# A sigmoid first on ScalarE, w_in's passes placed behind chosen sigmoids, and another split of the maxima between VectorE and ScalarE

## The chip, the cores and the metric

The kernel runs on one core of a Trainium2 chip. The metric is the device time of one execution in microseconds (us). Five engines work side by side, each through its own list of instructions in order: TensorE (PE, with its weight loads PEld), VectorE (DVE), ScalarE (ACT), GpSimd (POOL) and SyncE (SP), which here only issues DMAs. ACT issues some DMAs too. An instruction that waits for a semaphore holds everything behind it on its engine.

## The reference

Sigmoid attention with 12 heads over 8 batches of 448 tokens, then an MLP with a bent activation:

```python
scores = scale * np.matmul(q, k.transpose(0, 1, 3, 2)) - np.log(S)
attn = 1.0 / (1.0 + np.exp(-scores))
attn_out = np.matmul(attn, v)
x = attn_out.transpose(0, 2, 1, 3).reshape(B * S, H * D)
h = x @ w_in                       # 768 x 2048
g = np.where(h >= 1, h, np.where(h <= -1, 0.0, (h + 1) ** 2 / 4.0))
out = g @ w_out                    # 2048 x 768
```

q, k and v come as 32-bit floats, w_in and w_out as 64-bit floats, which the kernel receives as pairs of 32-bit words.

## The kernel before

Two heads make a pair (`p`), six pairs make a batch, and each pair has four pieces: three of 128 keys and a shorter one of 64. So batch 0 has 24 pieces, numbered 0 to 23, and batch 1 begins with piece 24. A piece is a score product (`psc`, L385), a sigmoid on ACT (`a`, L432) and a product with v (`pav`, L476). The first eight pairs are multiplied as 32-bit floats straight from their loads (`first_qvk` into `ghl`); the later ones (`qkv` into `raw`) are first split into a high and a low half-precision part (`hl`, L351 and L352, after maxima at L322) and rearranged by small DMAs into `qk`. When all pieces of a batch are through, `finish_x` finds the largest element of x (`xm`, L495 to L173), makes a scale `x_s` of it and splits x into high and low parts (`xhl`, L499 on ACT, L500 on DVE). Then the MLP runs: `up` (L700, 18 products for each of 16 chunks of d_ff), the bend of the activation (`g`, L713 to L717), `down` (L736). The attention of the next batch is spread between these products.

The weights come in 16 chunks each. A chunk's words land in a spare slot and go through a conversion pass by `Weight.convert`: an activation on ACT that reads the high words (L222), a shift and a merge with the low words on DVE (L228, L229), and the chunk's maximum. The maximum is found in one of two ways: on DVE (L233), or as the sum of absolute values on ACT (L215), which `find_scale` divides by the length. The chunks in `summed` go the second way: in the kernel before every second chunk of w_in (eight of them) and none of w_out. When the maxima of a group of eight chunks are there, `find_scale` makes its scale (`wi_s`, `wo_s`), and `split` makes a high part on ACT and a low part on DVE (L264, L265), or for the later chunks of w_in on POOL and ACT (L260 to L262).

Loads of w_in are issued by SP, one for each conversion pass; six of them fit into the spare slots, so load f + 6 waits for pass f on DVE. The first four loads of w_out are issued by SP as well, two when w_in's pass number 13 is written, two after its last; the rest are issued by ACT.

What sets the order: SP's list is written out by hand in the stage of batch 0 (`manual_schedule`). On the other engines a scheduler places the instructions by their priorities and its own estimate of times; the program's text only says where a step is offered. `keep_in_program_order` takes this freedom away for the instruction it is given. In the loop over the pieces the conversions before were offered at an even rate (the formula in `convert(wi, ...)`, with `WI_A` and `WI_B`), and the scheduler moved them.

## Time and profile before

| What | Value |
|---|---|
| median of 3 runs | 1182.82 us (1181.79 to 1187.88) |
| the profiled execution | 1182.99 us |
| its span in the trace | 1181.3 us |
| instructions | 20203 |
| mean granted TensorE clock | 0.987 of full |
| HBM read and written | 126.94 MB and 23.40 MB |

The span is the stretch from the first to the last recorded instruction; the time of the execution holds 1.69 us more around it. In the rows of the profile, "busy" is the time in which an engine executed something, and an idle time is put down to what ended it ("<-"). The names are those of the program's tiles; a line such as L432 is the line of the kernel printed above. A row of a timeline begins with the start and the duration in us and ends with the idle time ahead of it in brackets.

### The profile page before, as it was taken

The numbers are of one execution on the slowest core, as the hardware profiler recorded it, in microseconds if no ns is written. First come the engines' busy times: TensorE is split into PE (matmuls) and PEld (weight loads), VectorE is DVE, ScalarE is ACT, GpSimd is POOL, SyncE is SP. The second block draws the span as 40 slices with busy tenths as digits, with TensorE's granted clock in tenths as the row PEclk, the third lists the DMA queues.
The fourth block names the chain that finished last, engine by engine and source line by source line (L and its number), as shares of the span: only waits on it lengthen the run. The fifth ranks groups of instructions, "written<-read, shape, count | busy, mean of one in ns | idle before, by whom it ended". The sixth has DMA issues, their size and how long they took to land.

```text
span 1181.3 us, 20203 instructions
## 1 busy us (share of the span) xinstructions
PE 1146.3 (97%) x7662; PEld 669.0 (57%) x7662; DVE 824.9 (70%) x1760; ACT 697.1 (59%) x1158; POOL 321.6 (27%) x389
## 2 busy tenths in 40 slices
PE   5889999899999999999999999999999999999998
PEld 1224433344445776457755677457764677558954
DVE  4877999898945588467973689466883678736830
ACT  5975885665743587447763577546874486513410
POOL 0004310000332254325354236232534253310000
PEclk8899999899999999999999999999999999999999
DMA  9941544447532366224643165424552146302400
GB/s 361 335 150 61 195 149 132 151 142 244 176 109 64 119 213 212 64 64 150 253 146 100 33 251 193 132 64 141 196 207 68 61 155 223 117 25 98 153 16 32
DMA packets 58113, 170.01 MB, mean 144 GB/s; under 512 B 8608, under 2 KB 39840, under 8 KB 51872
## 3 DMA queue, kind: packets, MB, share of 16 engines
q1 hardware_dynamic: 56288, 159.29, 39.4%
q10 hardware_dynamic: 1728, 9.44, 2.3%
q8 instruction: 60, 0.98, 0.3%
q14 instruction: 37, 0.30, 0.1%
HBM read 126.94 MB, written 23.40 MB: 127 GB/s over the span
## 4 chain that ended last, share of the span: by engine, by line
PE 76%; DVE 9%; DMA 8%; ACT 4%; issue 1%; POOL 1%; SPq 0%; ACTq 0%; DVEq 0%
PE po L736 35%; PE ph L666 23%; PE pav L476 8%; PE psc L394 3%; PE psc L403 3%; DMA blocks<-mixs 2%; PE ph L700 2%; DMA w_out_sb<-w_in 2%; PE psc L389 1%; DMA raw<-qkv 1%; ACT a L432 1%; DVE g L714 1%; DMA w_out_sb<-w_out 1%; DMA w_in_sb<-blocks 1%; DVE mixs L624 1%
## 5 line engine op out<-in xcount | busy, mean ns | idle before, releaser
L736 PE MATMUL po<-ghl,w_out_sb 128*128 128x448 f16 x2304 | 445.7, 353 | 0.9 <-DVE g L715 0.9
L736 PEld LDWEIGHTS <-w_out_sb 128*128 128x128 f16 x2304 | 221.8, 98 | 216.6 <-issue 14.0
L666 PE MATMUL ph<-w_in_sb 128*128 128x224 f16 x3024 | 307.7, 259 | 2.0 <-DMA w_in_sb<-blocks 1.6
L666 PEld LDWEIGHTS <-w_in_sb 128*128 128x128 f16 x3024 | 282.6, 98 | 30.9 <-issue 27.4
L444 DVE SCALAR_TENSOR_TENSOR ahl<-psc,ahl 128x896 f16<-128x896 f32 (+1 forms) x170 | 152.9, 900 | 112.7 <-ACT ahl L443 110.4
L435 ACT ACTIVATE psc<-psc,nls,sqk 128x896 f32<-128x896 f32 (+1 forms) x136 | 129.4, 971 | 114.7 <-PE psc L403 97.2
L356 POOL TENSOR_SCALAR raw<-raw,qkv_s 128x448 f32<-128x448 f32 (+1 forms) x93 | 71.3, 781 | 452.9 <-DVE qkv_i L136 363.0
L443 ACT ACTIVATE ahl<-psc 128x896 f16<-128x896 f32 (+1 forms) x170 | 126.9, 762 | 32.9 <-DVE ahl L444 31.8
L700 PE MATMUL ph<-xhl,w_in_sb 128*128 128x448 f16 x576 | 115.5, 358 | 5.2 <-DVE xhl L500 2.9
L675 DVE TENSOR_TENSOR xhl<-ph,xhl 128x224 f32<-128x224 f32 x240 | 87.7, 382 | 26.2 <-PE ph L666 19.7
L322 ACT ACTIVATE dump<-raw 128x448 f16<-128x448 f32 (+1 forms) x105 | 61.8, 588 | 69.0 <-DMA raw<-qkv 68.0
L476 PE MATMUL pav<-ahl,v 128*64 128x448 f16 x748 | 95.6, 359 | 0.0
L713 ACT ACTIVATE g<-xhl,hr,ihr 128x448 f32<-128x448 f32 x96 | 68.7, 752 | 44.0 <-DVE xhl L675 43.1
L716 ACT ACTIVATE ghl<-g 128x448 f16<-128x448 f32 x128 | 72.7, 573 | 36.7 <-DVE g L715 36.3
L700 PEld LDWEIGHTS <-w_in_sb 128*128 128x128 f16 x576 | 55.9, 99 | 64.0 <-issue 16.4
L717 DVE TENSOR_TENSOR ghl<-g,ghl 128x448 f16<-128x448 f32 x128 | 85.6, 675 | 7.1 <-ACT ghl L716 6.6
L714 DVE SCALAR_TENSOR_TENSOR g<-g,rk 128x448 f32<-128x448 f32 x112 | 81.1, 739 | 10.7 <-ACT g L713 10.5
L746 DVE TENSOR_SCALAR o<-po,od 128x448 f32<-128x448 f32 x48 | 32.5, 679 | 65.8 <-PE po L736 65.6
L358 POOL TENSOR_TENSOR hl<-raw,hl 128x448 f16<-128x448 f32 x62 | 70.0, 1149 | 0.0
L394 PE MATMUL psc<-qk 128*128 128x448 f16 x252 | 66.6, 354 | 0.4 <-issue 0.3
L715 DVE SCALAR_TENSOR_TENSOR g<-xhl,ihs,g 128x448 f32<-128x448 f32 x96 | 65.5, 699 | 0.3
L385 PE MATMUL psc<-ghl 64*128 64x448 f32 (+1 forms) x128 | 37.4, 672 | 21.9 <-ACT a L432 17.1
(156 smaller groups left out, 1150.0 us busy)
## 6 DMA issues: line engine op xcount, KB each, us to landing
w_in_sb<-blocks SPq DMA_DIRECT2D x48, 1344.0 KB, 6.5
raw<-qkv SPq DMA_DIRECT2D x34, 704.0 KB, 4.9
qk<-hl SPq DMA_DIRECT2D x320, 56.0 KB, 2.0
w_out_sb<-w_in SPq DMA_DIRECT2D x16, 768.0 KB, 10.9
out_t<-o SPq DMA_DIRECT2D x48, 224.0 KB, 1.9
blocks<-mixs SPq DMA_DIRECT2D x8, 768.0 KB, 4.3
w_out_sb<-w_out ACTq DMA_DIRECT2D x6, 768.0 KB, 4.3
raww<-w_out ACTq DMA_DIRECT2D x6, 768.0 KB, 5.4
```

The source lines that it names most:

```text
L394: nc.tensor.matmul(out, kq[:, j, 1, w], kq[:, j, 0, :], start=True, stop=False)
L435: nc.scalar.activation(a, a, AF.Sigmoid, bias=nls, scale=sqk)
L443: nc.scalar.activation(hi, x, AF.Copy, scale=ATT)
L444: nc.vector.scalar_tensor_tensor(out=lo, in0=x, scalar=ATT, in1=hi, op0=ALU.mult, op1=ALU.subtract)
L476: nc.tensor.matmul(pav[j * D : (j + 1) * D, :S], *terms[j][t], start=c == 0 and t == 0, stop=mid and t == len(terms[j]) - 1,)
L666: nc.tensor.matmul(out, w[:, wt, wh, c * P : (c + 1) * P], xc[:, xt, c, xh, :], start=j in (0, 2) and c + wh + xh == 0, stop=c == HC - 1 a ...
L675: add = lambda out, q, other: nc.vector.tensor_tensor(out=out, in0=quarter(q), in1=other, op=ALU.add)
L700: nc.tensor.matmul(ph[:, :S], w_in_sb[:, f, wh, c * P : (c + 1) * P], xhl[:, c, xh, :], start=c == 0 and wh + xh == 0, stop=c == NCC - 1 a ...
L714: nc.vector.scalar_tensor_tensor(out=g, in0=g, scalar=rt, in1=g, op0=ALU.min, op1=ALU.mult)
L716: nc.scalar.activation(hi, g, AF.Copy)
L717: (nc.gpsimd if f % GPOOL else nc.vector).tensor_tensor(out=ghl[:, f, 1, :], in0=g, in1=hi, op=ALU.subtract)
L736: nc.tensor.matmul(po[:, :S], w_out_sb[:, f, wh, m * P : (m + 1) * P], ghl[:, f, gh, :], start=f == lo and wh + gh == 0, stop=f == hi - 1 ...
```

## The change

ACT gets a first instruction, a sigmoid of one column that nobody reads. The conversion passes of w_in are offered behind a list of sigmoids, `BEHIND`: pass f once the sigmoid of piece `BEHIND[f]` has been written, and the passes of w_in, the maxima of the first split pairs and all sums of w_out keep the order of the program among themselves. No chunk of w_in is summed any more, so DVE finds all 16 maxima; ten of the 16 chunks of w_out are summed on ACT, four passes behind their conversion. The group scale of w_in's first eight chunks is sought at piece 12 instead of 14, and the last pass and the second group's scale come right after batch 0's pieces.

```diff
-WI_A = 14
-WI_B = 5
+WI_A = 12
-WI_SUM = 2
-WO_SUM = 0
+SUMS = (), (0, 1, 2, 3, 4, 8, 9, 10, 11, 12)
+BEHIND = (1, 3, 4, 6, 7, 8, 10, 12, 13, 14, 16, 18, 19, 21, 22, 24)
+SUM_LAG = 4
...
-    nls = const.tile([P, 1], F32, name="nls")
+    nls = const.tile([P, 2], F32, name="nls")
     nc.vector.memset(nls, -math.log(S))
+    nc.scalar.activation(nls[:, 1:2], nls[:, 0:1], AF.Sigmoid)
+    nls = nls[:, 0:1]
...
-            mod = WI_SUM if name == "wi" else WO_SUM
-            self.summed = [f for f in range(NFC) if mod and f % mod == 0 and f not in (NA - 1, NFC - 1)]
+            self.summed = SUMS[name == "wo"]
...
+            f = self.at - SUM_LAG
+            if f in self.summed:
+                dump = wo.f32(-1) if self is wi else tmp_p.tile([P, S], F32, tag="tmp", name="dump").bitcast(F16)[:, :DM]
+                tc.keep_in_program_order(
+                    nc.scalar.activation(dump, self.f32(f), AF.Abs, accum_out=self.most[:, 1, f : f + 1])
+                )
             f = self.at - 2
             if 0 <= f < NFC:
-                w = self.words.pop(f)
-                if f in self.summed:
-                    dump = wo.f32(-1) if self is wi else w[:, :DM].bitcast(F32)
-                    nc.scalar.activation(dump, self.f32(f), AF.Abs, accum_out=self.most[:, 1, f : f + 1])
+                self.words.pop(f)
...
-                nc.scalar.activation(self.f32(f), high, AF.Prelu, scale=2.0**-112, alpha=-(2.0**32))
+                ins = nc.scalar.activation(self.f32(f), high, AF.Prelu, scale=2.0**-112, alpha=-(2.0**32))
+                if self is wi:
+                    tc.keep_in_program_order(ins)
...
-                    nc.scalar.activation(dump[:, : rt.shape[1]], rt, AF.Abs, accum_out=m[:, t : t + 1])
+                    ins = nc.scalar.activation(dump[:, : rt.shape[1]], rt, AF.Abs, accum_out=m[:, t : t + 1])
+                    if p < NFULL + 3:
+                        tc.keep_in_program_order(ins)
...
             scores([i])
+            convert(wi, sum(s <= i for s in BEHIND))
...
-            convert(wi, min((NA + 1) * at // WI_A, NA + 1 + max(0, at - WI_A) * (NFC - NA) // (NPIECE - WI_A + WI_B)))
+            convert(wi, sum(s < at + LAG for s in BEHIND))
...
         if wi.at < NFC + 1:
-            n = NPIECE - WI_A
-            convert(wi, NA + 1 + min(NFC - NA, (n + u + 1) * (NFC - NA) // (n + WI_B)))
-            if wi.at == NFC + 1:
-                wi.find_scale()
-                group_scales(0, inv_x, 1)
+            convert(wi, NFC + 1)
+            wi.find_scale()
+            group_scales(0, inv_x, 1)
```

The order of the built programs shows what becomes of it. The first place is SP's list near the end of batch 0's loads. In the kernel before, the last load of w_in is followed by eight rows of rearranging DMAs (`qk<-hl`, of which the last four are shown), and only then by the first two loads of w_out:

```order
L365 DMA qk<-hl 64x448
L366 DMA qk<-hl 64x448
L365 DMA qk<-hl 64x448
L366 DMA qk<-hl 64x448
L199 DMA w_out_sb<-w_out 128x1536 x2
L365 DMA qk<-hl 64x448
```

In the changed kernel the same stretch reads, from the load of w_in's chunk 14 on (the `ghl` rows are pairs 6 and 7):

```order
L200 DMA w_out_sb<-w_in 128x1536
L300 DMA ghl<-first_qvk 128x2x448
L301 DMA ghl<-first_qvk 128x448
L200 DMA w_out_sb<-w_in 128x1536
L300 DMA ghl<-first_qvk 128x2x448
L301 DMA ghl<-first_qvk 128x448
L200 DMA w_out_sb<-w_out 128x1536 x2
L373 DMA qk<-hl 64x448
```

The two loads of w_out moved ahead of the rearranging DMAs and follow the loads of w_in at once.

The second place is ACT's list where w_out's first chunk is converted. Before, it comes after the last pass and the last sum of w_in (the L215 row is that sum; `a` are the sigmoids, the L264 row a split of w_in):

```order
L222 ACTIVATE w_in_sb<-w_out_sb 128x768
L432 ACTIVATE a_324<-psc,nls 128x896
L264 ACTIVATE w_in_sb<-w_in_sb,wi_s 128x768
L482 ACTIVATE x_91<-pav 128x448
L215 ACTIVATE w_out_sb,wi_most<-w_in_sb 128x768
L222 ACTIVATE w_out_sb<-w_out_sb 128x768
L432 ACTIVATE a_331<-psc,nls 128x896
```

In the changed kernel it stands right behind the first maximum of pair 8 (L328), which follows the sigmoid of piece 21 (`a_378`); the sigmoids of pieces 22, 23 and 24 are `a_393`, `a_432` and `a_440`:

```order
L440 ACTIVATE a_378<-psc,nls 128x896
L328 ACTIVATE hl,m_382<-raw 128x448
L226 ACTIVATE w_out_sb<-w_out_sb 128x768
L490 ACTIVATE x_92<-pav 128x448
L270 ACTIVATE w_in_sb<-w_in_sb,wi_s 128x768
L328 ACTIVATE hl,m_382<-raw 128x448
L226 ACTIVATE w_in_sb<-w_out_sb 128x768
L226 ACTIVATE w_out_sb<-w_out_sb 128x768
L440 ACTIVATE a_393<-psc,nls 128x896
L440 ACTIVATE a_432<-psc,nls 128x448
L270 ACTIVATE w_in_sb<-w_in_sb,wi_s 128x768
L440 ACTIVATE a_440<-psc,nls 128x896
```

The pass over w_out's first chunk moved ahead of w_in's passes 13, 14 and 15 and of the last sigmoids that batch 0 needs.

The third place is DVE's list where the scale of x is made. Before, the chain from `xm` to `x_s` stands together, behind a split of w_in and a maximum of w_out:

```order
L265 SCALAR_TENSOR_TENSOR w_in_sb<-w_in_sb,wi_s 128x768
L233 TENSOR_REDUCE wo_most<-w_out_sb 128x1
L486 TENSOR_REDUCE xm<-x_91 128x1
L495 TENSOR_REDUCE xm_485<-xm 128x1
L162 TENSOR_SCALAR diag<-ident,xm_485 128x128
L173 TENSOR_REDUCE xm_485<-pm 128x1
L128 TENSOR_SCALAR x_e<-xm_485 128x1
L130 TENSOR_SCALAR x_e<-x_e 128x1
L132 TENSOR_SCALAR x_s<-x_e 128x1
```

In the changed kernel the second half of that chain (L175 to L134) comes behind w_out's passes 2 and 3 and mixes with the scale of w_in's second group:

```order
L271 SCALAR_TENSOR_TENSOR w_in_sb<-w_in_sb,wi_s 128x768
L360 SCALAR_TENSOR_TENSOR hl<-raw,qkv_s,hl 128x448 x2
L234 TENSOR_SCALAR w_out_sb<-w_out_sb 128x768
L271 SCALAR_TENSOR_TENSOR w_in_sb<-w_in_sb,wi_s 128x768
L235 SCALAR_TENSOR_TENSOR w_out_sb<-w_out_sb 128x768
L175 TENSOR_REDUCE xm_495<-pm 128x1
L175 TENSOR_REDUCE wi_x<-pm 128x1
L130 TENSOR_SCALAR x_e<-xm_495 128x1
L130 TENSOR_SCALAR wi_e<-wi_x 128x1
L132 TENSOR_SCALAR x_e<-x_e 128x1
L132 TENSOR_SCALAR wi_e<-wi_e 128x1
L134 TENSOR_SCALAR x_s<-x_e 128x1
```

Between the two halves of the chain there now stand the passes over w_out's chunks 2 and 3, two splits and the low parts of pair 9; and the scale of w_in's second group (`wi_x`, `wi_e`) moved forward from behind the first bends and takes turns with it.

## The prediction

> **What bounds the kernel now.** I read the page's busy times first, then the waits of TensorE, then the busy times by stage.
>
> ```profile
> PE 1146.3 (97%) x7662; PEld 669.0 (57%) x7662; DVE 824.9 (70%) x1760; ACT 697.1 (59%) x1158; POOL 321.6 (27%) x389
> PE psc L385 <- ACT a L432: 17.1, 8, 4.2
> PE psc L385 <- DMA ghl<-first_qvk: 4.5, 1, 4.5
> PE ph L700 <- DVE xhl L500: 2.9, 1, 2.9
> PE ph L700 <- DVE g L715: 1.9, 1, 1.9
> ```
>
> PE is busy for 97% of the span, so time can be won only where it waits. The rows of waits give the sum, the number of times and the longest: 21.6 of its 35 us of idling are waits for sigmoids and for the first load, and L385 stands only in the first eight pairs, that is in the first 84 us. So the question is when batch 0's attention ends and the first `up` can start. The stages (length, then busy time and count of PE, PEld, DVE, ACT and POOL, clock, DMA share, GB/s) and the place itself:
>
> ```profile
> 0.00:48.00 48.00, 31.54 (x110) 8.38 (x110) 29.21 (x54) 34.39 (x54) 0.70 (x6) 0.86 0.98 377
> 42.00:48.00 6.00, 4.23 (x20) 1.25 (x20) 5.56 (x10) 6.00 (x13) 0.00 (x0) 1.00 1.03 409
> 84.00:120.00 36.00, 35.87 (x184) 16.01 (x183) 28.88 (x67) 21.33 (x32) 15.43 (x12) 1.00 0.23 75
> 120.00:150.00 30.00, 29.93 (x153) 12.03 (x153) 28.30 (x46) 24.80 (x41) 7.93 (x6) 1.00 0.50 174
> 150.00:180.00 30.00, 29.93 (x147) 11.52 (x145) 28.53 (x59) 24.03 (x39) 3.93 (x3) 1.00 0.48 147
> ...
> 83.90 0.29 DVE L173 TENSOR_REDUCE xm<-pm 128x1 f32<-128x128 f32 x1 [1.98 <-PE pm L172]
> 84.60 0.15 DVE L132 TENSOR_SCALAR x_s<-x_e 128x1 int32<-128x1 int32 x1
> ...
> 87.50 6.98 PE L700 MATMUL ph<-xhl,w_in_sb 128*128 128x448 f16 x36
> 94.41 1.92 PE L385 MATMUL psc<-ghl 64*128 64x448 f32 x8
> ```
>
> Up to 48 us the DMA engines are full (share 0.98); from 84 us on PE is. `x_s` is there at 84.75 (84.60 + 0.15), the first `up` begins at 87.50. What the change wins or loses up to this point goes through to the end one for one, as long as nothing later starves PE.
>
> **The change, part by part.** *The sigmoid first.* Before, ACT waited for w_in's first words, then loaded a second table, and gave its first sigmoid after 11 us:
>
> ```profile
> 8.81 0.89 ACT L222 ACTIVATE w_in_sb<-w_out_sb 128x768 f32<-128x768 f32 x1 [6.73 <-DMA w_out_sb<-w_in]
> 9.72 1.28 ACT L432 ACT_TABLE_LOAD   x1
> ```
>
> Now the table load (1.28 us) lies under the first loads and piece 0 is weighed earlier, by 6.5 us at most (11.0 less the 4.5 at which the first load lets PE begin). I count this as nothing: the next paragraph shows that loads set the pace until 54 us, and an earlier start ends in the same wait.
>
> *The loads and the wait for w_out's first words.* ACT's list now has the pass over w_out's first chunk behind the sigmoid of piece 21, ahead of everything that batch 0 still needs. When do its words land? The DMA rows give KB for each issue:
>
> ```profile
> w_out_sb<-w_in SPq DMA_DIRECT2D x16, 768.0 KB, 10.9
> ghl<-first_qvk SPq DMA_DIRECT2D x8, 448.0 KB, 10.7
> ghl<-first_qvk SPq DMA_DIRECT2D x8, 224.0 KB, 9.3
> raw<-qkv SPq DMA_DIRECT2D x4, 448.0 KB, 8.3
> v<-qkv SPq DMA_DIRECT2D x3, 256.0 KB, 9.2
> ```
>
> Up to it SP has issued all of w_in (16 x 768), eight pairs (8 x 672), two `raw` (2 x 448), three `v` (3 x 256) and itself (768): 20,096 KB, or 20.6 MB. By 48 us 377 GB/s have brought 18.1 MB; the other 2.5 MB at the 409 GB/s of the row for 42 to 48 us take 6.1 us. So the words land at about **54.1 us** (56 if the next chunk, 0.79 MB, shares the engines to the end). ACT is there earlier: piece 21 is the 22nd, a piece costs PE 0.96 us for its scores (half the row at 94.41) and 0.86 for the product with v (half the row at 81.97, below), from 4.5 us on, and the mean clock of 0.86 costs up to 14% of 31.5, or 4.4 us, more; so its sigmoid ends near 49 us. Five us of waiting are new, and behind the waiting pass stand the sigmoids of pieces 22 to 29 and the passes 13 to 15. Before, those words were issued at 56.48 and ACT waited for later ones:
>
> ```profile
> 56.48 1.08 SPq L199 DMA_DIRECT2D w_out_sb<-w_out  x2
> 69.61 0.89 ACT L222 ACTIVATE w_out_sb<-w_out_sb 128x768 f32<-128x768 f32 x1 [2.67 <-DMA w_out_sb<-w_out]
> ```
>
> *From that wait to the scale of x.* Two queues run from 54.1 us; the longer sets `x_s`. DVE's list between the pass over w_out's chunk 0 and the chain of x holds, counted from the order of the built program, seven shifts, seven merges, three maxima, seven low parts of w_in, four low parts `hl`, two maxima of x and 17 small ones. Their means, and two neighbours of the timeline:
>
> ```profile
> L229 DVE SCALAR_TENSOR_TENSOR w_in_sb<-w_out_sb,w_in_sb 128x768 int32<-128x768 int32 x16 | 15.3, 957 | 0.4
> L265 DVE SCALAR_TENSOR_TENSOR w_in_sb<-w_in_sb,wi_s 128x768 f16<-128x768 f32 x9 | 9.1, 1015 | 0.8 <-ACT w_in_sb L264 0.7
> L228 DVE TENSOR_SCALAR w_in_sb<-w_in_sb 128x768 int32<-128x768 int32 x16 | 8.9, 556 | 16.5 <-ACT w_in_sb L222 16.3
> L233 DVE TENSOR_REDUCE wi_most<-w_in_sb 128x1 f32<-128x768 f32 x8 | 7.6, 952 | 0.2
> L486 DVE TENSOR_REDUCE xm<-x 128x1 f32<-128x448 f32 x6 | 3.7, 614 | 2.6 <-ACT x L482 2.6
> L352 DVE SCALAR_TENSOR_TENSOR hl<-raw,qkv_s,hl 128x448 f16<-128x448 f32 x4 | 2.6, 678 | 0.0
> ...
> 61.90 0.95 DVE L233 TENSOR_REDUCE wi_most<-w_in_sb 128x1 f32<-128x768 f32 x1
> 62.76 0.61 DVE L486 TENSOR_REDUCE xm<-x 128x1 f32<-128x448 f32 x1
> ```
>
> That is 3.9 + 6.7 + 2.9 + 7.1 + 2.7 + 1.2 and 17 x 0.16, together 27.2 us. Neighbours overlap by 0.09 us (61.90 + 0.95 less 62.76), 47 x 0.09 = 4.2, so 23 us if nothing depended on its neighbour, 27 if everything did; I take 25. ACT's list over the same stretch, with its own rows:
>
> ```profile
> L432 ACT ACTIVATE a<-psc,nls 128x896 f32<-128x896 f32 x21 | 21.2, 1008 | 2.7 <-PE psc L385 2.6
> L222 ACT ACTIVATE w_in_sb<-w_out_sb 128x768 f32<-128x768 f32 x16 | 14.4, 910 | 6.9 <-DMA w_out_sb<-w_in 6.7
> L264 ACT ACTIVATE w_in_sb<-w_in_sb,wi_s 128x768 f16<-128x768 f32 x9 | 8.5, 943 | 0.0
> L351 ACT ACTIVATE hl<-raw,qkv_s 128x448 f16<-128x448 f32 x4 | 2.5, 686 | 0.0
> L215 ACT ACTIVATE w_out_sb<-w_in_sb 128x768 f32<-128x768 f32 x8 | 6.8, 850 | 5.7 <-DVE w_in_sb L229 5.7
> ```
>
> Six long sigmoids, seven passes, seven splits and eleven short ones (at most 0.69) are 26.6 us, less about 0.1 us of overlap each 23.5; with about 1 us of waiting for w_out's chunk 2, 24.5. DVE is the longer by a little. So `x_s`: 54.1 + 0.8 (the pass on ACT) + 25 + 1.2 (the chain, 0.85 before, mixed with that of w_in's second group) = 81.1, and DVE puts 12 small instructions (12 x 0.15 less their overlap, about 1.5 us) and the first low part (0.6) ahead of PE's second product: the first `up` runs from **83.2 us**, 4.3 earlier than 87.50. PE has then also done pieces 30 and 31, the 1.9 us of the row at 94.41. Gain so far: 6.2 us.
>
> *The clock.* After piece 31's scores, at about 79.5 (54.1 + 24.5 + 0.9), PE has nothing to do until 83.2, a gap of 3.7 us. What such gaps cost:
>
> ```profile
> 72.27 0.98 PE L385 MATMUL psc<-ghl 64*64 64x448 f32 x4 [3.59 <-ACT a L432]
> 73.18 3.25 PE L476 MATMUL pav<-a,ghl 128*64 128x448 f32 x8
> 81.97 1.72 PE L476 MATMUL pav<-a,ghl 128*64 128x448 f32 x8
> 218.10 6.11 PE L700 MATMUL ph<-xhl,w_in_sb 128*128 128x448 f16 x18 [2.93 <-DVE xhl L500]
> ```
>
> After 3.59 us eight products took 3.25 instead of 1.72, 1.5 lost; after 2.93 us 18 took 6.11 instead of 3.49 (half of the row at 87.50), 2.6 lost. I take 2.3, between the two and nearer the second, since the same line L700 follows here. The Trainium skill, "TensorE: Matmul & The Clock Gate", Part 1, says that the clock halves after an idle window of about 3.4 us and recovers after as long a busy one; by that, an estimate, half a window is lost, 1.7, and the sum would be 0.6 us lower. The trace here loses more than that after a gap shorter than the window, so the rows decide.
>
> *The maxima.* Eight sums leave ACT before `x_s` and eight maxima join DVE; four w_out maxima leave DVE there. Behind `x_s`, DVE has 6 maxima less (6 x 0.95 = 5.7 us) and ACT ten sums more (10 x 0.85 = 8.5 us, by the row of L215). PE does not wait in 84 to 180 us, and ACT idles for 25.9 of the 96 us there (14.7, 5.2 and 6.0 by the rows), so I let both pass at nothing. Bounds: a gain of 5.5 if the later wait of 2.93 and its 2.6 of clock vanish with a freer DVE; a loss of 8.5 if every sum delays a bend. DVE's relief is spread well ahead of that wait, so zero is nearer than either.
>
> **Sum.** 4.3 + 1.9 - 2.3 = 3.9 us off the profiled execution's 1182.99: **1179.1 us**. It stands 0.17 us above the median of the runs, 1182.82, which changes nothing here.
>
> **Rivals.** *Faster: DVE's list does not hold `x_s`.* If its neighbours overlap as the lower bound has it and ACT passes its wait sooner, `x_s` falls to where ACT and PE allow, the first `up` comes about 3 us earlier, and the gap that cools PE is gone (2.3): 1173.8 us. For it: 23 against 24.5 us is within my bounds. Against it: each merge depends on its own shift, and the row of L228 shows DVE waiting on ACT's passes, 16.3 us.
>
> *Slower: the ten sums starve the bends.* They stand on ACT between loads that it issues itself, passes that wait for those loads, and the `g` that PE's next `up` needs. PE can run three `up` ahead (54 products, 10.5 us by the row at 87.50). If ACT falls behind by more than that, the 8.5 us come back on PE's path, with another cooling of 2.3: 1179.1 + 10.8 = 1189.9. Against it: the 25.9 us of idling.
>
> *No effect: the wait for w_out's words is longer.* Each us by which they land later than 54.1 moves everything behind by one. With 56 for the landing and DVE at its upper bound of 27, the 3.9 are gone: 1183.
>
> **How the numbers follow.** Forecast 1179.1 (1175 to 1184 for itself): 0.54. Faster rival 0.22, slower rival 0.11, no effect 0.13. About 0.5%, 5.9 us, is what a measurement of this kernel can tell from no change: below 1176.9 is faster, above 1188.7 slower. Faster: 0.22 and 0.08 from the forecast's lower edge, 0.30. Slower: 0.11. Same: 0.59. The range takes in the faster rival and stops short of the slower one: 1172.5 to 1186.5.
>
> **What would show it.** One table load on ACT, before 3 us. A wait of some 5 us on ACT for w_out's words ending near 54 to 56 us, with PE idle beside it. DVE without a gap from there to `x_s` near 81. The first `up` near 83, at half the clock at first. No new PE waits for `g` between 84 and 215 us, and the wait for `xhl` near 210 unchanged. The prediction is wrong if ACT's wait for w_out is short or missing, if DVE has gaps before `x_s`, or if sums on ACT are followed by PE waits.

## The result, and the profile after

The change makes the kernel slower: 1193.51 us in the median of 8 runs (1190.84 to 1196.39), against 1182.97 for 8 runs of the kernel before; the ratio is 1.0083, with a 95% interval of 1.0063 to 1.0102. That is outside the range of the prediction, above its upper end. The profiled execution of after took 1193.33 us, its span is 1191.6. First the page's busy times and the longest waits of TensorE (sum, times, longest, all in us), to be held against the same rows of before:

```profile
PE 1145.8 (96%) x7662; PEld 668.9 (56%) x7662; DVE 822.7 (69%) x1758; ACT 699.7 (59%) x1162; POOL 324.5 (27%) x389
PE pav L484 <- ACT x L490: 9.2, 1, 9.2
PE ph L708 <- DVE xhl L508: 4.4, 3, 3.3
PE psc L393 <- ACT a L440: 4.3, 5, 3.0
PE pm L158 <- DVE g L723: 3.6, 1, 3.6
PE psc L397 <- DVE ahl L452: 3.5, 2, 3.2
PE psc L402 <- DVE qkv_e L130: 2.4, 1, 2.4
```

TensorE's work is the same to half a us (1145.8 against 1146.3), so all 10.3 us of span are waiting. The waits for sigmoids in batch 0 have shrunk from 17.1 to 4.3 us, as the change meant; one wait of 9.2 took part of their place, and the rows that name VectorE are new or longer. Where they lie is read from the stages. First before, from 210 us, then after, from 84 us (length, then busy time and count of PE, PEld, DVE, ACT and POOL, clock, DMA share, GB/s):

```profile
210.00:240.00 30.00, 26.95 (x122) 10.96 (x121) 27.88 (x66) 18.68 (x27) 1.72 (x1) 0.89 0.33 126
300.00:330.00 30.00, 27.70 (x156) 13.50 (x154) 29.73 (x56) 19.93 (x35) 11.02 (x12) 1.00 0.68 223
```

```profile
84.00:120.00 36.00, 33.50 (x170) 15.40 (x169) 30.21 (x48) 21.80 (x33) 23.46 (x17) 0.99 0.12 36
210.00:240.00 30.00, 20.57 (x91) 8.44 (x92) 25.28 (x63) 17.63 (x25) 1.64 (x1) 0.85 0.30 119
300.00:330.00 30.00, 24.05 (x127) 11.12 (x126) 29.61 (x52) 20.70 (x33) 9.95 (x11) 0.95 0.52 171
```

After loses 6.4 us of TensorE's time at 210 to 240 us and 3.7 at 300 to 330, stages in which no line was changed. VectorE, too, is less busy at 210 to 240 us (25.28 against 27.88), so the two wait for each other there.

**Batch 0 took the forecast course, 1 to 1.5 us late.** The rows of after for the steps of the prediction, from the timelines of ScalarE, VectorE and TensorE (start, length, and in brackets the idle time before it and what ended it):

```profile
0.80 1.28 ACT L101 ACT_TABLE_LOAD   x1 [0.80 <-PEq L944]
55.30 0.88 ACT L226 ACTIVATE w_out_sb<-w_out_sb 128x768 f32<-128x768 f32 x1 [8.32 <-DMA w_out_sb<-w_out]
56.68 3.25 PE L484 MATMUL pav<-a,ghl 128*64 128x448 f32 x8 [9.23 <-ACT x L490]
80.83 3.40 PE L393 MATMUL psc<-ghl 64*128 64x448 f32 x8 [2.98 <-ACT a L440]
82.49 0.15 DVE L134 TENSOR_SCALAR x_s<-x_e 128x1 int32<-128x1 int32 x1
84.17 4.73 PE L708 MATMUL ph<-xhl,w_in_sb 128*128 128x448 f16 x23
99.25 12.82 PE L708 MATMUL ph<-xhl,w_in_sb 128*128 128x448 f16 x66 [1.45 <-DVE g L723]
```

ScalarE waits 8.32 us for w_out's first words, TensorE 9.23 beside it; `x_s` is there at 82.64 (82.49 + 0.15), and batch 0's first `up` starts at 84.17 us, where before had 87.50. VectorE's longest gap between the words and `x_s` is 0.80 us, so that its list did set this stretch.

**Where it was lost.** Two points of TensorE's row tell the story: its first `down` stands at 166.62 us before and at 164.84 after, 1.8 earlier; batch 2's first product stands at 390.44 before and at 400.61 after, 10.2 later. The whole loss lies between them. Batch 1's turn, on TensorE, before and then after:

```profile
214.42 0.74 PE L700 MATMUL ph<-xhl,w_in_sb 128*128 128x448 f16 x3
224.81 6.42 PE L700 MATMUL ph<-xhl,w_in_sb 128*128 128x448 f16 x33
235.08 0.18 PE L156 MATMUL pm<-mb,one 128*128 128x3 bf16 x1
235.38 13.78 PE L700 MATMUL ph<-xhl,w_in_sb 128*128 128x448 f16 x72
```

```profile
213.15 0.73 PE L708 MATMUL ph<-xhl,w_in_sb 128*128 128x448 f16 x3 [0.55 <-ACT xhl L507]
217.21 6.95 PE L708 MATMUL ph<-xhl,w_in_sb 128*128 128x448 f16 x27 [3.33 <-DVE xhl L508]
224.09 0.38 PE L402 MATMUL psc<-qk 128*64 128x448 f16 x2
224.71 4.71 PE L708 MATMUL ph<-xhl,w_in_sb 128*128 128x448 f16 x24
236.31 0.16 PE L158 MATMUL pm<-mb,one 128*128 128x3 bf16 x1 [3.58 <-DVE g L723]
237.83 12.14 PE L708 MATMUL ph<-xhl,w_in_sb 128*128 128x448 f16 x54 [1.36 <-DVE g L723]
```

Before, TensorE does 21 products of `up` (3, and 18 after its wait of 2.93 us), then scores, then 33, then scores and products with v, then the small product for q, k and v (L156), and 72 more without a wait. After, the order is another: 30 products (3 and 27), then the scores. What stands behind those scores is seen on ScalarE and VectorE of after. (A mix, `mixa` and `mixs`, joins two chunks of w_in to the blocks with which the later batches multiply; VectorE and ScalarE make the eight mixes between the rest of their work.)

```profile
224.82 0.73 ACT L440 ACTIVATE a<-psc,nls,sqk 128x448 f32<-128x448 f32 x1 [3.19 <-PE psc L411]
226.18 0.93 ACT L631 ACTIVATE mixs<-mixa,mixes 128x768 f16<-128x768 f32 x1
230.24 1.96 ACT L721 ACTIVATE g<-ph,hr,ihr 128x448 f32<-128x448 f32 x3 [1.27 <-DVE hr L542]
```

```profile
213.74 1.83 DVE L618 TENSOR_TENSOR mixa<-w_in_sb 128x768 f32<-128x768 f16 x2 [2.79 <-DMA blocks<-mixs]
227.14 1.68 DVE L632 SCALAR_TENSOR_TENSOR mixs<-mixa,mixes,mixs 128x768 f16<-128x768 f32 x1 [1.83 <-ACT mixs L631]
230.00 0.14 DVE L542 TENSOR_SCALAR hr<-rk 128x1 f32<-128x1 f32 x1
233.25 1.82 DVE L618 TENSOR_TENSOR mixa<-w_in_sb 128x768 f32<-128x768 f16 x2
235.58 0.68 DVE L723 SCALAR_TENSOR_TENSOR g<-ph,ihs,g 128x448 f32<-128x448 f32 x1
```

As these rows read, it is a ring of queues that each issue in their order. ScalarE's sigmoid waits 3.19 us for scores that stand behind 30 products; behind it stands the high part of a mix (L631); VectorE waits 1.83 us for that, and behind its wait stand batch 1's scales (`hr`); ScalarE waits 1.27 us for `hr` before the first `g`; and TensorE waits 3.58 us, because the small product of L158 needs the tile of PSUM, the memory that TensorE writes, that this `g` (L723) frees. VectorE's own list adds to the last link: between the second step of that `g` (L722, at 232.06 us) and the third (L723, at 235.58) stand the first two adds of the next mix. Idle at 213 to 238 us: 0.55 + 3.33 + 3.58 + 1.36 = 8.8 us, where before had 2.93.

At 300 us it comes again. VectorE waits for a mix's buffer, then is late for what TensorE needs (`qkv_e`, the first step of the scales of q, k and v; `ahl`, sigmoids split into high and low parts):

```profile
298.27 1.83 DVE L618 TENSOR_TENSOR mixa<-w_in_sb 128x768 f32<-128x768 f16 x2 [2.45 <-DMA blocks<-mixs]
311.01 0.16 DVE L130 TENSOR_SCALAR qkv_e<-psc 128x3 f32<-128x3 f32 x1
```

```profile
296.92 0.18 PE L158 MATMUL psc<-mb,one 128*128 128x3 bf16 x1
311.22 0.54 PE L402 MATMUL psc<-qk 128*128 128x448 f16 x2 [2.45 <-DVE qkv_e L130]
325.56 0.73 PE L397 MATMUL psc<-hl,w_in_sb 128*128 128x448 f16 x3 [3.22 <-DVE ahl L452]
```

A tile that TensorE filled at 296.92 us with the small product for q, k and v is read by VectorE at 311.01, 14.1 us later (10.4 in before, from 292.46 to 302.84, where TensorE did not wait for it). TensorE needs the tile for its next scores and waits 2.45 us, and 3.22 at the next such place, for `ahl`.

None of this code was edited. The kernel is built with an order that a scheduler finds by simulating a time line, so that another batch 0 gave it another simulated time at every later choice: on VectorE the two kernels' orders differ up to about row 550 of 1,760, on TensorE up to about 330 us, and from there they are the same again.

### The profile page after: what moved, and what is told of

It reads as the page before. It is cut to its first block, busy times and chain, and to the rows that moved or that the text cites. A ratio compares the mean times of both kernels' runs of the same rounds, so it can differ in the third digit from the quotient of the medians.

```text
span 1191.6 us, 20214 instructions
## 1 busy us (share of the span) xinstructions
PE 1145.8 (96%) x7662; PEld 668.9 (56%) x7662; DVE 822.7 (69%) x1758; ACT 699.7 (59%) x1162; POOL 324.5 (27%) x389
## 4 chain that ended last, share of the span: by engine, by line
PE 71%; DVE 3%; DMA 2%; ACT 1%; issue 1%; ACTq 0%; DVEq 0%; SPq 0%
PE po L744 32%; PE ph L674 24%; PE pav L484 7%; PE psc L402 3%; PE psc L411 2%; PE psc L397 1%; PE ph L708 1%; DMA w_in_sb<-blocks 1%; DMA raw<-qkv 1%; DMA blocks<-mixs 1%; DVE mixa L618 0%; DVE ahl L452 0%; DVE g L722 0%; DVE mixs L632 0%; ACT psc L443 0%
## 5 line engine op out<-in xcount | busy, mean ns | idle before, releaser
L708 PE MATMUL ph<-xhl,w_in_sb 128*128 128x448 f16 x576 | 119.3, 363 | 8.0 <-DVE xhl L508 4.4
L328 ACT ACTIVATE dump<-raw 128x448 f16<-128x448 f32 (+1 forms) x105 | 62.0, 590 | 71.0 <-DMA raw<-qkv 70.0
L722 DVE SCALAR_TENSOR_TENSOR g<-g,rk 128x448 f32<-128x448 f32 x112 | 82.0, 748 | 10.7 <-ACT g L721 10.5
L723 DVE SCALAR_TENSOR_TENSOR g<-xhl,ihs,g 128x448 f32<-128x448 f32 x96 | 65.6, 700 | 0.3
L484 PEld LDWEIGHTS <-v 128*64 128x64 f16 x748 | 36.4, 109 | 38.1 <-issue 23.5
```

The source lines that it names most:

```text
L484: nc.tensor.matmul(pav[j * D : (j + 1) * D, :S], *terms[j][t], start=c == 0 and t == 0, stop=mid and t == len(terms[j]) - 1,)
L708: nc.tensor.matmul(ph[:, :S], w_in_sb[:, f, wh, c * P : (c + 1) * P], xhl[:, c, xh, :], start=c == 0 and wh + xh == 0, stop=c == NCC - 1 a ...
L722: nc.vector.scalar_tensor_tensor(out=g, in0=g, scalar=rt, in1=g, op0=ALU.min, op1=ALU.mult)
```

## The experiments

Two theories. **O (order):** the loss is in the order dealt anew at batch 1's turn, and what batch 0 gained is still there. **S (sums):** the ten sums on ScalarE, and what they delay, cost it. Each run's numbers are in one table; the first `down` shows what batch 0 gained, batch 2's first product what is left of it. The ratios are to before, with their 95% intervals. Each run's line numbers are its own. Before's own median was 1182.97 to 1184.85 us in the sets of runs behind these ratios, so rows of different sets are compared by ratio; the places in us are of one profile each.

| run | first `down`, us | batch 2, us | median, us | ratio |
|---|---|---|---|---|
| before (profiled) | 166.62 | 390.44 | | |
| after | 164.84 | 400.61 | 1193.51 | 1.0083 (1.0063 to 1.0102) |
| after_old_turn | 164.57 | 389.00 | 1184.47 | 1.0008 (0.9994 to 1.0021) |
| before_new_turn | 167.50 | 404.06 | 1195.69 | 1.0102 (1.0083 to 1.0121) |
| no_out_sums | 167.66 | 390.65 | 1185.23 | 1.0008 (0.9992 to 1.0024) |
| mix_behind_scales | 166.00 | 390.76 | 1183.86 | 1.0002 (0.9987 to 1.0016) |
| mix_spread_after | 165.23 | 388.32 | 1181.44 | 0.9995 (0.9981 to 1.0008) |
| mix_spread_before | 167.21 | 391.11 | 1184.49 | 1.0013 (1.0003 to 1.0024) |
| spread_no_sigmoid | 165.72 | 389.30 | 1183.11 | 1.0003 (0.9991 to 1.0015) |
| spread_out_pass_later | 165.95 | 390.56 | 1183.44 | 1.0006 (0.9994 to 1.0018) |
| after_old_pe | 165.56 | 390.22 | 1184.48 | 0.9999 (0.9987 to 1.0011) |
| after_old_dve | 165.55 | 392.04 | 1185.44 | 1.0005 (0.9994 to 1.0016) |
| spread_adds_on_pool | 166.26 | 391.02 | 1185.87 | 1.0015 (1.0001 to 1.0029) |
| sum_lag_5 | 165.22 | 394.65 | 1187.79 | 1.0039 (1.0023 to 1.0055) |
| spread_passes_later | 154.26 | 379.81 | 1172.26 | 0.9917 (0.9890 to 0.9944) |
| passes_later_old_turn | 154.79 | 379.17 | 1172.03 | 0.9904 (0.9886 to 0.9921) |
| passes_later_free | 154.09 | 387.01 | 1180.72 | 0.9977 (0.9966 to 0.9989) |

**The two crosses.** TURN is a table with, for each engine, the places (counted from the program's end) of its instructions in the order in which the other kernel issues them: 260 on VectorE, 170 on ScalarE, 1,700 on TensorE. Each is tied behind the one ahead of it in its queue; no wait is added. Ahead of the turn the orders are those of the kernel itself, behind it those of the other.

```diff
+    for engine, places in TURN.items():
+        these = by[engine]
+        for one, two in zip(places, places[1:]):
+            tc.add_manual_dep(
+                these[-1 - two], these[-1 - one].name,
...
```

> The kernel after, with one thing forced: from the scales of x for batch 1 on (about 208 us), VectorE, ScalarE and TensorE issue their work in the order that the kernel before has there; ahead of that point the order is that of after. Theory O (order): the 10 us are lost in the order that the scheduler dealt anew at batch 1's turn (208 to 345 us); what batch 0 gained stays. Then TensorE keeps its lead of 1.5 to 2.5 us over before as far as the wait on the mixes lets it: 1180 to 1184 us, ratio to before 0.997 to 1.001. Theory S (sums): the ten sums on ScalarE and what they delay cost it, wherever the later work stands: 1190 to 1194, ratio 1.006 to 1.010.

> The cross of the first: the kernel before, with the order of after forced on VectorE, ScalarE and TensorE from batch 1's scales of x on. Theory O: it loses what after lost there, 8 to 12 us: 1191 to 1195 us, ratio 1.007 to 1.010, with TensorE waiting for g near 236, for the scales of q, k and v near 311 and for ahl near 325 us. Theory S: no sums were moved, so 1182 to 1184, ratio 1.00.

Measured: 1184.47 us and 1195.69. TensorE's small product and scores in before_new_turn:

```profile
240.25 0.17 PE L163 MATMUL pm<-mb,one 128*128 128x3 bf16 x1 [3.58 <-DVE g L722]
316.20 0.54 PE L401 MATMUL psc<-qk 128*128 128x448 f16 x2 [2.43 <-DVE qkv_e L135]
330.54 0.73 PE L396 MATMUL psc<-hl,w_in_sb 128*128 128x448 f16 x3 [1.58 <-DVE ahl L451]
```

The order alone carries the loss: given to before, which has none of the sums, it brings the same waits of 3.58 and 2.43 us; taken from after, which keeps its sums, it takes them away. S falls, O stands for the loss. But O's second half, that the gain of batch 0 is still there, is not borne out: after_old_turn is 0.5 us above its range, level with before, though it came to the turn 2.9 us ahead (first `up` of batch 1 at 211.50 against 214.42). It waits longer there:

```profile
216.81 5.31 PE L715 MATMUL ph<-xhl,w_in_sb 128*128 128x448 f16 x18 [4.58 <-DVE rt L549]
```

4.58 us in place of 2.93, since VectorE's own list behind the mix (213.3 us, against 214.6) is hardly earlier. So of the lead of 2.9 us 1.4 are left at batch 2 (389.00 against 390.44). That is the profile, which took 1182.14 us, the shortest of this run's ten; in the medians nothing is left (1184.47 against 1184.17 for before in the same set).

**Which engine's order.** The same table, for one engine alone; the scheduler deals the others anew.

> The kernel after with the order of before forced on TensorE alone, from batch 1's first up on; VectorE and ScalarE are dealt anew by the scheduler. If TensorE's own order holds the loss (where its scores for batch 2 and its small products for scales stand between the ups): 1181 to 1186 us, ratio to before 0.998 to 1.003. If VectorE's order holds it: 1188 to 1194.

> The kernel after with the order of before forced on VectorE alone, from batch 1's scales of x on; TensorE and ScalarE are dealt by the scheduler, TensorE differently from before as from after. If VectorE's order holds the loss: 1181 to 1186 us, ratio 0.998 to 1.003. If TensorE's order holds it, or what counts is that the engines' orders fit each other: 1188 to 1196.

Measured: 1184.48 and 1185.44 us: both recover. In after_old_pe, where the scores stand behind 21 products again, the small product at 235.78 us has no wait in place of 3.58, and the wait of 1.36 behind it is 0.61:

```profile
236.57 13.78 PE L713 MATMUL ph<-xhl,w_in_sb 128*128 128x448 f16 x72 [0.61 <-DVE g L728]
```

The ring accounts for a part of this: the first `g` is done 2.1 us sooner (234.13 against 236.26 us), and TensorE itself comes 3.1 us later to the place (235.86 against 232.73), mostly because 18 products at a low clock took 6.47 us. In after_old_dve the wait is still there, 3.57 at 234 us, without the ring: the scores stand ahead of the products there and ScalarE's sigmoid has no wait. VectorE has other work, 2.2 us of it, between the second and the third step of the first `g`. The waits of 2.45 and 3.22 near 311 and 325 us are one of 0.46 at 317 and one of 1.89 at 320. So the ring is one way in which that `g` came late, not the only one. As the other engines are dealt anew in both runs, they don't show whether one engine's order or the fit of the orders was wrong in after. The expectation for after_old_dve had put the fit at 1188 to 1196 us, and that did not come.

**Another deal of the same change**, with the sums of w_out on ScalarE one step later:

```diff
-SUM_LAG = 4
+SUM_LAG = 5
```

> The kernel after with SUM_LAG 5 in place of 4: each sum on ScalarE is written one pass later, and nothing else is changed or forced. The scheduler then deals batch 1's turn differently from after and from before. If the 10 us belong to the one deal that after drew: 1181 to 1186 us, ratio to before 0.997 to 1.002. If the changed batch 0 makes a freely dealt turn bad in general: 1189 to 1195.

Measured: 1187.79 us, between the two expectations, 1.0039. TensorE's wait for `g` at the turn is 1.56 in place of 3.58, and the scores' is 1.56 at 319 us. So deals differ by steps of some us, and after drew a bad one, not the only bad one.

**No sums of w_out on ScalarE.**

```diff
-SUMS = (), (0, 1, 2, 3, 4, 8, 9, 10, 11, 12)
+SUMS = (), ()
```

> The kernel after with all 16 maxima of w_out on VectorE (no sums on ScalarE); the order is left to the scheduler, and at batch 1's turn it comes out almost as in before. Theory O: 1180 to 1184 us, the lead of batch 0 kept and no waits for g near 236 us. Theory S: the same or lower, since no sum is left on ScalarE; so alone it tells only that sums are not needed for the gain, and it has to be read with the first run.

Measured: 1185.23 us, 1.2 above the range, and the lead of batch 0 is not kept: its first `down`, at 167.66 us, is 1.0 later than in before. With all maxima on VectorE the first `up` comes at 86.31 us, its first 54 products take 12.99 us, and three waits of TensorE for ScalarE and VectorE come to 3.0 us. So it is the sums that make the change gain in batch 0: 2.8 us by these two profiles (167.66 less 164.84), 2.2 against the mean of the seven with after's order (165.43). In the time of the kernel it does not show: from batch 1's scales on this run has before's order, as after_old_turn has, which keeps its sums, and both stand at 1.0008.

**The mixes at the turn.** VectorE's part of each mix but the first behind the last of batch 1's scales:

```diff
+    turned = state["last"]
...
-                        mix(mixed_at)
+                        with tc.issue_after(turned.ins) if mixed_at else ExitStack():
+                            mix(mixed_at)
```

> The kernel after, where VectorE's part of the mixes from the second on must stand behind the last small instruction of batch 1's scales; the rest is left to the scheduler. Theory O, mechanism: at the turn VectorE, which issues in order, stands 2.8 us at a mix that waits for a transfer, with the low halves of x and the scales for the first g behind it. With the mix behind them, the waits of 3.3 us for xhl at 217 and of 3.6 us for g at 236 go, and their half clock: 1193 less 6 to 10, 1183 to 1187 us if the waits at 311 and 325 us stay, 1179 to 1182 if they go too. If the mix is not what holds VectorE there, nothing changes: 1191 to 1195.

Measured: 1183.86 us. The wait for `xhl` is gone, TensorE's first 54 products stand without a gap from 213.44 us, and it comes to the next products with v 7.8 us ahead of before (223.98 against 231.77). A wait of 2.62 for `g` is still there, against the expectation, though the scales no longer stand behind a mix. By 322 us the lead is lost, with a wait of 1.54 for `qkv_e` at 299 and one of 3.39 for `ahl`:

```profile
230.09 13.78 PE L708 MATMUL ph<-xhl,w_in_sb 128*128 128x448 f16 x72 [2.62 <-DVE g L723]
314.64 1.28 PE L397 MATMUL psc<-hl,w_in_sb 128*128 128x448 f16 x3 [3.39 <-DVE ahl L452]
```

**The mixes spread.** The first add of each mix but the first is kept behind what is written ahead of it on VectorE, and the mixes reach to unit 100. With this edit, before and after have the same order on the three engines from the turn (200 us) to the end, so that the pair compares batch 0 alone.

```diff
-MIX1 = 85
+MIX1 = 100
...
+            if i:
+                tc.keep_in_program_order(add)
```

> The kernel after, where the first add of each mix from the second on is kept behind everything written ahead of it on VectorE, and the eight mixes are spread over units 8 to 100 in place of 8 to 85. Theory O with its mechanism (VectorE is what TensorE waits for at the turn and again near 300 to 327 us, and the mixes are what fills it there): no wait for xhl or g over 1 us at 213 to 240 us, and the lead is still there at 330 us, because mixes now stand past it: 1175 to 1180 us, ratio to before 0.992 to 0.997. Rival: VectorE's work of the stage binds wherever the mixes stand, and a lead at the turn is lost by 330 us, as in the run with the mix behind the scales: 1182 to 1186, ratio 1.000.

> The kernel before with the same edit of the mixes. From batch 1's scales of x on its order on VectorE, ScalarE and TensorE is the same as that of mix_spread_after, so that the two differ by what the change does in batch 0 alone. If batch 0's lead of 1.5 to 2.5 us (seen at 150 us) passes on one for one, as the prediction had it, this takes 1.5 to 2.5 us more than mix_spread_after; if a later wait swallows it, the two are equal within 0.7 us.

Measured: 1181.44 and 1184.49 us. The pair passes batch 0's lead on, as the prediction had said of the whole change: 2.0 us at the first `down`, 2.8 at batch 2's first product, 0.0018 (2.1 us) between the ratios, whose intervals just overlap, and 3.1 in the medians, above the 1.5 to 2.5 expected. Against before, mix_spread_after, between its two expectations, is no faster: its lead of 9.0 us at batch 1's last `up` (309.88 against 318.85 us) is 2.1 at batch 2's start, because the mixes now stand where batch 2's scales are due.

```profile
366.25 0.23 PE L174 MATMUL psc<-diag,one 128*128 128x128 bf16 x1 [3.12 <-DVE diag L164]
```

**Two parts of batch 0**, on mix_spread_after: the sigmoid at the start left out, and w_out's first pass kept behind what is written ahead of it on ScalarE, 15 instructions later.

```diff
-    nc.scalar.activation(nls[:, 1:2], nls[:, 0:1], AF.Sigmoid)
...
-                if self is wi:
+                if self is wi or f == 0:
                     tc.keep_in_program_order(ins)
```

> mix_spread_after without the sigmoid at ScalarE's start (the table is loaded before the first pass needs it, as before); the order from the turn on is the same. The prediction counted this part at nothing, because loads set the pace until 54 us: TensorE's place at 150 us and the time equal to mix_spread_after within 0.5 us. Rival: the first sigmoid comes 4.5 to 6.5 us earlier and part of it stays: 1 to 3 us slower than mix_spread_after.

> mix_spread_after, where the pass over w_out's first chunk is kept behind everything written ahead of it on ScalarE, 15 instructions later (4 sigmoids, 3 passes and 4 splits of w_in among them). If ScalarE's wait of 8.3 us for these words at 47 to 55 us is what sets the end of batch 0's attention, the wait falls under 2 us, TensorE does not stand 9.2 us there, and the first up comes 2 to 5 us earlier: 2 to 5 us off mix_spread_after. If VectorE's list sets it, TensorE waits later for the same time: equal within 1 us.

Measured: 1183.11 and 1183.44 us, both with intervals that overlap that of mix_spread_after; the first `down` is 0.5 and 0.7 us later. The medians are 1.7 and 2.0 us above it, so that the sigmoid by itself may be worth nothing or the rival's 1 to 3 us. Without it, too, ScalarE comes to the wait for w_out's words, which takes up an earlier start; what the sigmoid is worth where that wait is gone was not run. The second run doesn't decide what it was made for. Only the first chunk's pass was kept back; the pass over the second stands 4 instructions further on, and took over the wait:

```profile
57.91 0.89 ACT L226 ACTIVATE w_out_sb<-w_out_sb 128x768 f32<-128x768 f32 x1 [7.24 <-DMA w_out_sb<-w_out]
```

No sigmoid had passed it, so whether the loads set the pace up to there, as the prediction has it, or the place of the pass in ScalarE's row, stayed open until the last three runs below.

**Adds on GpSimd**, on mix_spread_after:

```diff
-MIXP = 0
+MIXP = 2
```

> mix_spread_after with the first two adds of each mix on GpSimd in place of VectorE (16 adds of 0.95 us, 15 us of VectorE's work from 175 to 360 us). If VectorE's load binds batch 1's stage, as the waits of TensorE for VectorE at 228, 309 and 350 to 366 us in mix_spread_after say, most of the 6 us of idling and lost work there go: 1174 to 1179 us, ratio 0.992 to 0.997. Rival: the adds take longer on GpSimd, VectorE waits for them in its order, or both engines slow each other: 1181 to 1187.

Measured: 1185.87 us; the rival held. An add takes 1.81 us there in the median (16 of them), against 0.95 on VectorE, and VectorE's row has 6.8 us of waits for them.

**The passes over w_out behind the work at hand.** The same tie for the first three chunks of w_out: each pass keeps the place on ScalarE at which the program writes it, which for the first is 13 instructions later. The first of the runs has it on mix_spread_after; the second on after, with before's order from batch 1's scales on (TURN, as above); the third on after alone, where the scheduler deals the turn itself.

```diff
-                if self is wi:
+                if self is wi or f < 3:
                     tc.keep_in_program_order(ins)
```

> mix_spread_after, where the passes over w_out's first three chunks are kept behind what is written ahead of them on ScalarE: the first of them 13 instructions later, behind 3 more sigmoids, 3 splits and 2 passes of w_in (in spread_out_pass_later the pass over the second chunk was left free and took over the wait, 4 instructions later, so no sigmoid passed it). If the place of these passes is what makes TensorE wait 9 us at 48 to 57 us, ScalarE's wait for w_out's words falls from 8 to under 3 us, TensorE's wait of 9 falls alike, and the first up comes 2 to 5 us earlier; first down 160 to 163 us in place of 165.2, 2 to 4 us off mix_spread_after. If the loads set the pace up to about 56 us whatever stands where, TensorE waits as long for other things (w_in's last words, the sigmoids behind their passes): first down within 0.8 us of 165.2 and the time equal.

> after_old_turn with the passes over w_out's first three chunks kept later, as in spread_passes_later (there the first down came at 156.6 us, 10 ahead of before); the order from batch 1's scales of x on is that of before. If batch 1's turn holds TensorE by VectorE's mix only as far as that mix comes earlier too, a lead of 10 us is more than the turn can swallow: 1174 to 1179 us, ratio 0.992 to 0.997. If the turn swallows a lead of any size: 1182 to 1186.

> The kernel after with the same three passes kept later and nothing else changed or forced; the scheduler deals batch 1's turn much as in after. If the ring at the turn is a matter of that order, as the crosses say, it is there again, and the 10 us of batch 0 and the 10 lost at the turn come to 1181 to 1187 us. If more room ahead of the turn breaks the ring: 1172 to 1178.

Measured: 1172.26, 1172.03 and 1180.72 us; the first two are 2 us and more below what their better theory expected. (The expectation of passes_later_old_turn has spread_passes_later's first `down` at 156.6 us; its profile has 154.26, as in the table.) The pass over the first chunk, on ScalarE in spread_passes_later, and TensorE's wait at that place in passes_later_old_turn, with that run's busy times from 84 to 150 us (length, then the engines as above):

```profile
56.06 0.91 ACT L226 ACTIVATE w_out_sb<-w_out_sb 128x768 f32<-128x768 f32 x1
```

```profile
60.09 0.97 PE L400 MATMUL psc<-ghl 64*64 64x448 f32 x4 [3.84 <-ACT a L447]
```

```profile
84.00:150.00 66.00, 66.00 (x333) 28.37 (x330) 53.77 (x106) 47.95 (x78) 17.07 (x14) 1.00 0.36 118
```

The words are there when the pass comes: ScalarE has no wait, where after has 8.32 us, and has meanwhile done sigmoids and passes that stood behind it. TensorE waits 3.84 us in place of 9.23; the first `up` comes at 76.84, 77.26 and 76.03 us in the three (84.17 in after), the first `down` 10 to 11 us earlier than in after. So 7 to 8 us are won by the first `up`; most of the rest are waits behind it, since TensorE idles for 2.5 us of 84 to 120 us in after and for none of the row above. So what held TensorE and ScalarE up to 56 us was the place of the passes, not the loads, which SP issues at the same time (w_out's first at 45.43 us in after, 45.57 in spread_passes_later).

What becomes of a lead of that size is seen in the last two. In before's order the lead over before is 12.7 us where batch 1's `up` begins (201.72 against 214.42) and 11.3 at batch 2 (379.17 against 390.44): it goes through but for 1.4 us, as much as the profile of after_old_turn lost of its small lead. In the medians 11.8 us arrive (1172.03 against 1183.78). The turn takes its part in one longer wait:

```profile
207.34 5.63 PE L715 MATMUL ph<-xhl,w_in_sb 128*128 128x448 f16 x18 [4.90 <-DVE xhl L515]
```

In the freely dealt order the lead is 12.0 us at batch 1's first `up` (202.39) and 3.4 at batch 2 (387.01). The long waits are back, for `xhl`, for `g` and, 3.33 us at 312.66, for `ahl`:

```profile
206.52 11.86 PE L708 MATMUL ph<-xhl,w_in_sb 128*128 128x448 f16 x51 [3.40 <-DVE xhl L508]
225.58 0.17 PE L158 MATMUL pm<-mb,one 128*128 128x3 bf16 x1 [2.25 <-DVE g L723]
```

The ring is not what makes them here: the scores stand behind all 54 products, but ScalarE has their sigmoid (221.58 us) behind the first step of `g` (219.75), and no part of a mix waits for it. Between the second and the third step of the first `g` VectorE has an add of a mix again.

passes_later_old_turn and spread_passes_later beat both kernels: by 0.96% and 0.83% against before, and after is 1193.51 us against their 1172.

## Why the prediction was wrong

- **The step that failed** is the one that carried the gain to the end: "What the change wins or loses up to this point goes through to the end one for one, as long as nothing later starves PE." Its condition did not hold. I tested it on 84 to 180 us, where TensorE does not wait, and took the rest as it was, "the wait for `xhl` near 210 unchanged". The crosses show that the order there was changed and costs 9 us (1.0083 against 1.0008) to 12 (1.0102 against before). With before's order forced the profiles lose 1.4 us of a lead on the way, of the small one of after_old_turn and the large one of passes_later_old_turn alike; in the medians the large one arrives (11.8 us) and nothing can be seen of the small one (1184.47 against 1184.17). With the mixes spread a small lead does arrive. So a lead is not passed on one for one by itself: it depends on the order at the turn.
- **The table first.** Right: one load, at 0.80 us. Counted at nothing, and in the run without it nothing can be told from 0; that run still has the wait for w_out's words.
- **The wait for w_out's words.** Right in kind and place, too short: they were used at 55.30 us in place of 54.1, ScalarE stood from 46.98 and not from 49, so 8.3 us and not 5. What failed here as well is the cause, that "loads set the pace until 54 us": they do so only while the pass stands ahead of the sigmoids of pieces 22 to 29, and moving three passes back was worth 10 us by the first `down`. The prediction had named the queue behind the pass, but took its wait for one that the loads would impose anyway.
- **`x_s` and the first `up`.** 82.64 us in place of 81.1, and 84.17 in place of 83.2: 1.2 of the 1.5 come from the later words. From their use to `x_s` it took 27.3 us, where the prediction's terms give 27.0.
- **The clock and what follows the first `up`.** Forecast 2.3 us lost. Of the 3.3 us of the earlier first `up` and the 1.9 of pieces already done, 1.8 are left at the first `down`, so 3.4 were lost. The gap, of 2.98 us and not 3.7, came ahead of the scores of pieces 30 and 31, not behind them: these eight products took 3.40 where 1.92 is full speed, 1.5 lost, and the first `up` ran at full clock but for its start. To this come waits of 0.52, 0.52 and 1.45 us for low parts of x and for `g`, which I had not counted; with them the account is 0.6 too long.
- **The maxima.** Counted at nothing, with bounds of +5.5 and -8.5. no_out_sums puts the sums at a gain of 2.2 to 2.8 us in batch 0, and after_old_turn shows no loss from them later. The size was off, the bounds held it.
- **Batch 0 in all.** Forecast 3.9 us; the first `down` in the seven profiles with after's order up to there stands at 165.43 us in the mean, in the three with before's at 167.11: 1.7 us, less than half. Without the change of order, too, the time would have been nearer to before's than forecast.
- **The rivals.** "The ten sums starve the bends" came nearest in time (1189.9), and for the wrong reason. The bends were late, but by VectorE's mixes, and before_new_turn has the same waits without a sum. "The wait for w_out's words is longer" had its wait, yet batch 0 gained all the same. No rival held a change of order.
- **The signs named.** "No new PE waits for `g` between 84 and 215 us" failed at 99.25 us, by 1.45. The wait for `xhl` near 210 was nearly unchanged (3.33 against 2.93), and the table load, ScalarE's wait and VectorE's list without gaps came as said, so the signs of batch 0 could not warn; the decisive waits, at 236 and 311, lie past the stretch that I had chosen to watch.

Open: which single choices of the scheduler make the loss. The ring at 213 to 238 us and the late reading of the tile near 311 are read from the trace; neither was moved alone, and the wait for `g` also stands where the ring does not.

## What to carry to other kernels

Where a scheduler deals the order by simulated times, an edit is also a new deal of everything behind it: compare the built order of all engines to the end of the difference, not only around the edit, and look at each place where engines wait for one another. To learn what an edit is worth, tie the rest to one order in both kernels; here that turned a loss of 0.8% into no change for the same edit. On an engine that issues in order, work that waits for a late load belongs behind the work that is ready: three conversions moved back by a dozen places took 8 us of ScalarE's waiting away and brought 1% of this kernel's time (0.9904 against 1.0008, in the same order behind them).

## What was not expected of the hardware

A subtraction on GpSimd holds VectorE up. At the turn of before, and then of after (GpSimd's subtraction, VectorE's instruction):

```profile
224.15 1.72 POOL L262 TENSOR_TENSOR w_out_sb<-w_out_sb 128x768 f16<-128x768 f32 x1 [18.41 <-ACT w_out_sb L261]
224.29 2.39 DVE L624 SCALAR_TENSOR_TENSOR mixs<-mixa,mixes,mixs 128x768 f16<-128x768 f32 x1
226.36 1.64 POOL L268 TENSOR_TENSOR w_out_sb<-w_out_sb 128x768 f16<-128x768 f32 x1 [21.29 <-ACT w_out_sb L267]
```

VectorE's low part of a mix takes 1.01 us in the median, 2.39 when it starts 0.14 us behind the subtraction, and 1.68 (the row at 227.14 above) when 0.78 behind. The Trainium skill, "SBUF — State Buffer", section "Who interferes with whom", says that a VectorE instruction with two inputs in SBUF and a GpSimd instruction that reads SBUF share a port, and that the later one is blocked until the first ends. By that, an estimate, they would take 2.59 (225.87 less 224.29, and 1.01) and 1.87 us; the traces agree within 0.2.

What a gap costs the clock has two sizes here. In after 27 products took 6.95 us behind the gap of 3.33, where 72 at full speed took 13.78, so 5.17 for as many: 1.8 lost. In before 18 took 6.11 behind one of 2.93: 2.6 lost. The granted clock, read in steps of 0.2 us, stood at 0.50 for 3.4 us in the first (217.6 to 221.0) and for 6.8 in the second (216.5 to 223.3). It stood there for 6.8 us, too, at after's next place (234.6 to 241.4); TensorE had no products of `up` for the first half of that, and the 54 behind it, which took 12.14 us where 10.34 is full speed, lost 1.8. In each, half of what TensorE works through at 0.50 is lost. So the 2.3 of the prediction stood between two cases, and the runs don't show what decides between them. Half a window, 1.7 us, was the prediction's estimate by the Trainium skill, "TensorE: Matmul & The Clock Gate", Part 1; the traces agree where the low stretch is 3.4 us long, and not where it is 6.8.
